# Few-slot experts computed two parts at a time, and the last expert's few-slot tile moved behind the first block's angles

## The chip, the cores and the metric

The kernel runs on one core of one Trainium2 chip. The metric is the time of one execution in microseconds (us); three executions of the kernel before are given, and one further execution was profiled.

## What is computed

Three layers run in one launch: attention with a local window and a few global keys (8 heads, 768 positions, head size 64, batch 2), a mixture of 8 experts in which each of the 1,536 tokens goes to one expert, and a layer that mixes tokens by angles. The change touches the second layer and its border with the third.

```python
# experts: token (b, s) belongs to expert e, with probability p[e]
h = np.maximum(x[b, s] @ w1[e], 0.0)          # 512 -> 1024
out[b, s] = p[e] * (h @ w2[e])                # 1024 -> 512
...
# third layer
theta = x @ w_theta
zr, zi = x * np.cos(theta), x * np.sin(theta)
y = np.einsum('ts,bsd->btd', w_tok_r, zr) + np.einsum('ts,bsd->btd', w_tok_i, zi)
u = x + y
out = u + np.maximum(u @ w_ch, 0.0)
```

All is in float32. A product of two float32 matrices is made in one of two ways: of raw float32 operands in one matmul (which the profile records as two), or of operands split into a high and a low part of type fp32r (three matmuls: high by high, high by low, low by high).

## The kernel before

**Ranks and slots.** The experts are ranked by their number of tokens. Rank r has room for `RCAP[r]` = 288, 256, 256, 256, 192, 192, 160, 160 tokens, in tiles of 128 slots: three tiles for rank 0, two for the others. A last tile with 32 (ranks 0, 6, 7) or 64 (ranks 4, 5) slots is a few-slot tile. `FEW` = 192 is the room up to which the first product of a rank uses raw weights.

**Units.** The 1,024 hidden columns of an expert are cut into 8 parts of 128; one rank and one part are a unit, u = 8 r + f, 64 units in all. For each unit TensorE (PE) runs `mm1(u + 2)` (tokens by w1: 12 fp32r matmuls in ranks 0 to 3, 4 raw ones in ranks 4 to 7), then `mm2(u)` (hidden by w2: for each full tile three fp32r matmuls of 512 columns; for the few-slot tile raw matmuls that put 32 or 64 slots on 32 or 64 columns of the array, 4 or 2 of them side by side, L1501). `relu` makes the hidden parts: ScalarE (ACT) the high part `hh`, VectorE (DVE) the low part `hl` and, for a few-slot tile, the raw `hx`. `split_w1` and `split_w2` split the weights on ACT and DVE. Between these steps `tick` does small steps of the jobs that convert the third layer's 64-bit tables (26 jobs, six steps each, five of them with one DVE operation; `JRATE[r]` steps per unit, until unit `JL`).

**Loads.** SyncE (SP) loads a piece, which is the w1 and the w2 part of two units, 512 KB each, into three buffers each (`raw1`, `raw2`). The next load of a buffer is issued when the last reader of the old piece is done. `x_tr` transposes the tokens of the next rank.

**The border.** After unit 63 `y_last` scales both tiles of rank 7 (full tile on DVE, L1550; few-slot tile on ACT, L1551) and stores them to `yd` with two SP transfers (L1552, L1553). `first_put` puts the first block of 128 tokens together on PE without waiting for the store; then come its angles (L1823), its transposes back (L1827), 8 `keep_warm` matmuls whose result nobody reads (`W0`, L1809), and `h_tr(1)`, the transposes of the second block, which a gather (`gather_y`, on GpSimd, POOL) reads back from `yd`. Then the mix of the first block (L1746) begins.

The order of all instructions is written out by hand: each engine runs its list in the order of the code.

Of the kernel before, what the change touches and what calls it, by code (L numbers as in the profile page):

```python
# [38 lines left out]
FEW = 192  # L39
RBASE = [1, 4, 6, 8, 10, 12, 14, 16]  # L40
NSLOT = 18
LONG = 128 + RCAP[0]
# [22 lines left out]
JRATE = (0, 1.3, 1.3, 1.3, 2.4, 2.4, 2.4, 2.4)  # L65
# [6 lines left out]
JL = 61  # L72
W0, W1 = 8, 0
LOADS = ((1, 1), (0, 2), (1, 2), (2, 1), (2, 2))
# [19 lines left out]
def kernel(  # L94
# [341 lines left out]
    with ExitStack() as actx:  # L436
# [366 lines left out]
        def experts_slots():  # L803
# [20 lines left out]
            V.tensor_scalar(flag_i, ordf[:, 1, 0:1], gA[0:1], None, op0=ALU.max)  # L824
# [10 lines left out]
            V.scalar_tensor_tensor(yidx, slotf[:, 0], 128.0, slotf[:, 1], op0=ALU.add, op1=ALU.add)  # L835

# [142 lines left out]
    xgs, pieces, regs = {}, {}, {}  # L979
    NPC = 32  # L980

    def load_piece(n, parts=(1, 2)):
# [4 lines left out]
        k = r if n else -1  # L987
        if k not in regs:
            regs[k] = SP.value_load(order_g[0:1, r : r + 1] if n else first_i, min_val=0, max_val=E - 1)
        ev = regs[k]  # L990
        p = pieces.setdefault(n, {})
        if 2 not in p and 2 in parts:
            p[2] = pre.tile([128, 2, DM], F32, tag="raw2", name="raw2", bufs=NRAW)
# [34 lines left out]
    slot0 = ct([128, 1], F32, "slot0")  # L1028

# [247 lines left out]
    wsp1, mb_, pR_ = {}, [], []  # L1277
# [9 lines left out]
    def x_tr(r, i, low=True):  # L1287
# [8 lines left out]
        tp = (pR_[0] if r else pZ).tile([128, 4, 128], F32, tag="tr", name="tr")  # L1296
# [45 lines left out]
    with ExitStack() as mctx:  # L1342
# [5 lines left out]
        pR_.append(pR)  # L1348
        pslot = {}
# [11 lines left out]
        def gather_p(r, i):  # L1361
            n = RBASE[r] + i
            pslot[n] = mb.tile([128, 1], F32, tag="ps", name="ps", bufs=6)
# [36 lines left out]
        def first_put():  # L1400

            outs = first["xT"] = [pB.tile([128, 2, 128], F32, tag="b", name="first") for _ in range(2)]
            for n, (rows, pick) in enumerate(((first["rows"], ident), (first["yo"][0], first["hitT"]))):
# [21 lines left out]
        hts = {}  # L1425

        hps = {}

        def mm1(u):
# [4 lines left out]
            hp = pB.tile([128, 512], F32, tag="b", name="h")  # L1434
            if N <= FEW:
                x, o = f32(xTs[r][0]), u % 2
# [10 lines left out]
            else:  # L1447
                h1, l1 = wsp1.pop(u)
# [6 lines left out]
            hps[u] = hp  # L1455

        def relu(u):
            if u >= 64:
                return
            r = u // 8  # L1460
            N = RCAP[r]
            hp = hps.pop(u)
            hh = mb.tile([128, max(RCAP)], F32R, tag="hh", name="hh", bufs=4)
            hl = mb.tile([128, max(RCAP)], F32R, tag="hl", name="hl", bufs=4)
            n, hx = N // 128 * 128, None
            if width(r, RTILES[r] - 1) == 128:
                n = N
            A.activation(hh[:, :n], hp[:, :n], AF.Relu)  # L1468
            if n < N:

                hx = mb.tile([128, 64], F32, tag="hx", name="hx", bufs=4)
                V.tensor_scalar(hx[:, : N - n], hp[:, n:N], 0.0, None, op0=ALU.max)
            V.scalar_tensor_tensor(hl[:, :n], hp[:, :n], 0.0, f32(hh[:, :n]), op0=ALU.max, op1=ALU.subtract)  # L1473
            hts[u] = (hh, hl, hx)

        yps = {}

        def mm2(u):
            r, f = divmod(u, 8)
            if f == 0:  # L1480
                yps[r] = [pO.tile([128, DM], F32, tag="o", name="o") for _ in range(RTILES[r])]
            h2, l2, w = wsp2.pop(u)
            hh, hl, hx = hts.pop(u)
            for i in range(RTILES[r]):
                lo = i * 128
                M = min(128, RCAP[r] - lo)
                out = yps[r][i]
                c = width(r, i)
                if c == 128:
# [8 lines left out]
                else:  # L1498
                    W = 4 * c
                    for g in range(128 // c):  # L1500
                        PE.matmul(  # L1501
                            out[g * c : g * c + M, :W],
                            lhsT=hx[:, :M],
                            rhs=w[:, g * W : (g + 1) * W],
                            start=(f == 0),
                            stop=(f == 7),
                        )
            if u % 2:
                pieces.pop(u // 2)
                load_piece(u // 2 + NRAW, (2,))  # L1510

        def y_out(u):
# [32 lines left out]
        def y_last():  # L1545
            r, w = E - 1, width(E - 1, 1)
# [8 lines left out]

        mm1(0)
        relu(0)
        mm1(1)
        split_w1(2)
        split_w2(0)  # L1560
        relu(1)
        jstate["eng"], jstate["sub"] = A, V
# [428 lines left out]
```

## Time and profile before

| | us |
|---|---|
| median of three runs | 497.88 |
| lowest, highest | 496.69, 499.67 |
| the profiled execution, whole | 495.95 |
| its span, first to last instruction | 494.1 |
| PE busy in the span | 478.5 |
| DVE busy | 353.8 |
| ACT busy | 260.8 |

The profile lists for each engine when an instruction began, what it waited for, and how long it took. A matmul record is pipelined: records overlap, so the time of a step is read from start to start of what follows it. PEld is the loading of the stationary operand, which goes on beside the matmuls.

### The profile page before, as it was taken

The numbers are of one execution on the slowest core, as the hardware profiler recorded it, in microseconds if no ns is written. First come the engines' busy times: TensorE is split into PE (matmuls) and PEld (weight loads), VectorE is DVE, ScalarE is ACT, GpSimd is POOL, SyncE is SP. The second block draws the span as 40 slices with busy tenths as digits, with TensorE's granted clock in tenths as the row PEclk, the third lists the DMA queues.
The fourth block names the chain that finished last, engine by engine and source line by source line (L and its number), as shares of the span: only waits on it lengthen the run. The fifth ranks groups of instructions, "written<-read, shape, count | busy, mean of one in ns | idle before, by whom it ended". The sixth has DMA issues, their size and how long they took to land.

```text
span 494.1 us, 9501 instructions
## 1 busy us (share of the span) xinstructions
PE 478.5 (97%) x3328; PEld 385.0 (78%) x3330; DVE 353.8 (72%) x955; ACT 260.8 (53%) x634; POOL 117.4 (24%) x145
## 2 busy tenths in 40 slices
PE   8998998899999999999999999999999999999994
PEld 4676776678788899987777776888888888888884
DVE  6878878857665878777777888657999795751421
ACT  5977786732455756665455664555655354520300
POOL 4003214234105303021311102303453232430400
PEclk9999999999999999999999999999999999999999
DMA  8967578713949876976888995420012000000122
GB/s 244 350 191 247 178 242 248 227 44 114 337 63 299 287 255 227 303 253 225 297 278 288 305 312 174 142 98 22 23 64 72 15 23 21 2 34 32 34 96 69
DMA packets 62343, 83.18 MB, mean 168 GB/s; under 512 B 6496, under 2 KB 40928, under 8 KB 62288
## 3 DMA queue, kind: packets, MB, share of 16 engines
q1 hardware_dynamic: 53812, 61.97, 39.4%
q10 hardware_dynamic: 5708, 13.50, 8.0%
q0 software_dynamic: 2768, 7.02, 4.6%
q8 instruction: 28, 0.46, 0.4%
q14 instruction: 27, 0.22, 0.1%
HBM read 71.14 MB, written 11.34 MB: 167 GB/s over the span
## 4 chain that ended last, share of the span: by engine, by line
PE 79%; DVE 7%; DMA 6%; ACT 4%; issue 2%; ACTq 0%; SPq 0%; DVEq 0%; POOLq 0%
PE a L1746 21%; PE o L1491 11%; PE h L1454 8%; PE b L1783 7%; PE th L1670 6%; PE h L1438 6%; PE s L547 3%; PE x L626 3%; PE o L1501 3%; PE pt L602 2%; DVE sm L569 2%; DMA yd<-yo 2%; DMA jraw<-in_w_tokT_dram 2%; PE h L757 2%; PE y L768 2%
## 5 line engine op out<-in xcount | busy, mean ns | idle before, releaser
L1746 PE MATMUL a<-wtokr,z 128*128 128x512 f32 x480 | 87.1, 340 | 0.0
L1746 PEld LDWEIGHTS a<-wtokr,z 128*128 128x128 f32 x480 | 73.5, 188 | 10.7
L1491 PE MATMUL o<-w2s,hh 128*128 128x512 f32 x192 | 64.9, 417 | 0.7 <-DVE w2s L1422 0.4
L579 ACT ACTIVATE pr<-sm,st 128x256 f32<-128x256 f32 (+1 forms) x96 | 46.1, 482 | 19.9 <-DVE st L569 19.9
L1422 DVE TENSOR_TENSOR w2s<-raw,w2s 128x512 fp32r<-128x512 f32 x64 | 44.0, 688 | 14.7 <-ACT w2s L1421 14.6
L1454 PE MATMUL h<-xT,w1s 128*128 128x256 f32 (+1 forms) x384 | 53.4, 288 | 1.2 <-DVE w1s L1325 0.6
L1454 PEld LDWEIGHTS h<-xT,w1s 128*128 128x128 f32 x384 | 49.5, 188 | 4.3 <-DVE w1s L1325 1.1
L1438 PE MATMUL h<-xT,raw 128*128 128x192 f32 (+1 forms) x256 | 46.0, 323 | 0.0
L1438 PEld LDWEIGHTS h<-xT,raw 128*128 128x128 f32 x256 | 38.5, 190 | 7.0 <-issue 6.6
L1421 ACT ACTIVATE w2s<-raw 128x512 fp32r<-128x512 f32 x64 | 39.9, 623 | 7.6 <-ACT yo L1537 3.5
L569 DVE CUSTOM_DVE_ANT_0 sm<-s,bias 128x256 f32<-128x256 f32 (+1 forms) x96 | 34.0, 395 | 10.3 <-PE s L547 10.1
L1468 ACT ACTIVATE hh<-h 128x256 fp32r<-128x256 f32 (+1 forms) x64 | 20.8, 324 | 33.8 <-PE h L1454 18.9
L1491 PE MATMUL o<-w2s,hl 128*128 128x512 f32 x96 | 38.0, 395 | 0.0
L1491 PEld LDWEIGHTS o<-w2s,hh 128*128 128x128 f32 x192 | 33.0, 189 | 5.2 <-DVE w2s L1422 1.2
L1012 POOL DMA_INDIRECT xg<-xd,xidx x17 | 16.8, 986 | 85.0 <-PE tr L1299 78.6
L602 PE MATMUL pt<-ident,pr 128*128 128x128 f32 x176 | 26.0, 280 | 4.5 <-DVE xt L652 3.2
L1325 DVE TENSOR_TENSOR w1s<-raw,w1s 128x512 fp32r<-128x512 f32 x32 | 22.1, 690 | 9.6 <-ACT w1s L1324 9.4
L1791 DVE SCALAR_TENSOR_TENSOR ob<-b,xTf 128x512 f32<-128x512 f32 (+1 forms) x16 | 8.8, 556 | 27.6 <-PE b L1783 27.5
L1702 POOL TENSOR_TENSOR si<-si,yg 128x512 f32<-128x512 f32 x10 | 13.4, 1343 | 60.0 <-ACT si L1695 50.8
L1473 DVE SCALAR_TENSOR_TENSOR hl<-h,hh 128x256 fp32r<-128x256 f32 (+1 forms) x64 | 22.4, 350 | 6.0 <-ACT hh L1468 6.0
L602 PEld LDWEIGHTS pt<-ident,pr 128*128 128x128 f32 x176 | 19.2, 141 | 9.4 <-DVE xt L652 3.8
L547 PE MATMUL s<-kall,q 64*128 64x256 f32 (+1 forms) x192 | 25.6, 385 | 0.0
(266 smaller groups left out, 951.3 us busy)
## 6 DMA issues: line engine op xcount, KB each, us to landing
raw<-in_w_dram SPq DMA_DIRECT2D x64, 512.0 KB, 5.2
vv<-in_pack_dram SPq DMA_DIRECT2D x10, 512.0 KB, 5.7
jraw<-in_w_tokT_dram ACTq DMA_DIRECT2D x10, 512.0 KB, 4.7
w<-in_w_dram SPq DMA_DIRECT2D x16, 256.0 KB, 6.6
kall<-in_pack_dram SPq DMA_DIRECT2D x10, 320.0 KB, 4.4
xd<-xt SPq DMA_DIRECT2D x12, 256.0 KB, 2.1
q<-in_pack_dram SPq DMA_DIRECT2D x11, 256.0 KB, 4.5
yd<-yo ACTq DMA_DIRECT2D x11, 256.0 KB, 4.1
```

The costliest lines, as they stand in the source:

```text
L547: PE.matmul(sp[hh][:, 0:W], lhsT=qs[n][half, j], rhs=kall[half, b, j, t * 160 + 160 - W : t * 160 + 160], start=True, stop=True,)
L569: V.tensor_tensor_reduce(out=sm[:, hh, 0:W], in0=ust[u]["s"][hh], in1=bias[:, 2 * j + hh], scale=-0.125, scalar=BIG, op0=ALU.add, op1=ALU.min,
L579: A.activation(pr[:, hh, 0:W], sm[:, hh, 0:W], AF.Exp, bias=st[:, hh : hh + 1], scale=-1.0, accum_out=sums[n][:, 2 * j + hh : 2 * j + hh + 1],
L602: PE.transpose(pt[:, hh, c], pr[:, hh, c * 128 : (c + 1) * 128], ident)
L1421: A.activation(h2, bb[:, o], AF.Copy)
L1422: V.tensor_tensor(l2, bb[:, o], f32(h2), op=ALU.subtract)
L1438: PE.matmul(hp[:, :N], lhsT=pieces[u // 2][1][:, j, o * 128 : (o + 1) * 128], rhs=x[:, j, :N], start=(j == 0), stop=(j == 3),)
L1454: PE.matmul(hp[:, :N], lhsT=wa[:, j], rhs=xa[:, j, :N], start=(k == 0), stop=(k == 11))
L1491: PE.matmul(out[:M], lhsT=ha[:, lo : lo + M], rhs=wa, start=(f == 0 and q == 0), stop=(f == 7 and q == 2),)
L1670: PE.matmul(th, lhsT=xa[:, j], rhs=wa[:, j], start=(n == 0), stop=(n == 11))
L1746: PE.matmul(acc[b][d][o], lhsT=za[:, d * 128 : (d + 1) * 128], rhs=wa[:, lo:hi], start=(t == 0 and n == 0 and (o == 0 or d % 2 == 0)), sto ...
L1783: PE.matmul(op[:, : hi - lo], lhsT=wa[:, d, e * 128 : (e + 1) * 128], rhs=ua[d][:, lo:hi], start=(n == 0), stop=(n == 11),)
```

## The change

Three things change, and some numbers with them.

1. Ranks 4 to 7 are computed two units at a time: `mm1` of two units, `mm2` of two units, then the few-slot matmuls of both (`mm2_few`). One PSUM tile holds the hidden columns of both units, so `relu` is one ACT and two DVE instructions for the two. The few-slot tile of rank 0 too is computed once per two units.
2. The few-slot tile of rank 7 is not computed there. Its hidden parts are kept in `y0`, its raw w2 is loaded into the place of the third layer's `wch` table (`late`), and its 32 matmuls (`y_few`) stand in the place of the 8 `keep_warm` matmuls. Its store follows the first part of the mix, and the gathers of blocks 1 to 3 stand before it. The first block's split parts `xh`, `xl` move from `wch` to tiles of their own.
3. That is allowed where no token of the first four blocks of the first batch lies in that tile: the flag that starts the general path now also rises when the last expert has more than 128 tokens in the first seven blocks (five small DVE instructions in place of one in `experts_slots`).

The numbers: `JRATE` and `JL` (job steps per unit), the order of the first loads (`LOADS`: the w2 part of piece 0 goes ahead of the w1 part of piece 1), and in unit 0 `mm2(0)` stands ahead of `mm1(2)`.

```diff
-JRATE = (0, 1.3, 1.3, 1.3, 2.4, 2.4, 2.4, 2.4)
+JRATE = (0, 1.4, 1.4, 2, 2.3, 2.3, 1.8, 0.6)
-JL = 61
-W0, W1 = 8, 0
-LOADS = ((1, 1), (0, 2), (1, 2), (2, 1), (2, 2))
+JL = 59
+LOADS = ((0, 2), (1, 1), (1, 2), (2, 1), (2, 2))
...
+        if 2 in parts and n >= NPC - 4:
+            if n % 2 == 0:
+                late[0] = res.tile([128, 4, DM], F32, tag=f"wch{n // 2 % 2}", name="late")
+            p[2] = late[0][:, n % 2 * 2 : n % 2 * 2 + 2]
+        elif 2 not in p and 2 in parts:
...
             if N <= FEW:
-                x, o = f32(xTs[r][0]), u % 2
+                if o == 0:
+                    hps[u] = pB.tile([128, 2, 256], F32, tag="b", name="h")
+                hp = hps[u - o][:, o]
...
+        def mm2_few(u, out=None):
+            r = u // 8
+            i = RTILES[r] - 1
+            c, M, out = width(r, i), RCAP[r] - i * 128, out or yps[r][i]
+            for v in (u, u + 1):
+                hx, w = fews.pop(v)
+                for g in range(128 // c if c < 128 else 0):
+                    PE.matmul(out[g * c : g * c + M, : 4 * c], lhsT=hx[:, :M], ...
...
+        def y_few():
+            out = pA_[0].tile([128, 512], F32, tag="a", name="few")
+            yield
+            for u in range(8 * E - 8, 8 * E, 2):
+                mm2_few(u, out)
+            yield
+            W, M = 4 * width(E - 1, 1), RCAP[E - 1] - 128
+            yo = y0[:, 384 : 384 + W]
+            A.activation(yo, out[:, :W], AF.Copy, scale=pslot.pop(RBASE[E - 1] + 1))
+            SP.dma_start(groups_out(YLAST + 128, M, W), yo)
...
-            mm1(u + 2)
-            mm2(u)
...
+            if RCAP[r] > FEW:
+                if u:
+                    mm1(u + 2)
+                mm2(u)
+                if u % 2:
+                    mm2_few(u - 1)
...
+            elif u % 2 == 0:
+                mm1(u + 2)
+                mm1(u + 3)
+                if f == 2 and r < 7:
+                    for i in range(2):
+                        x_tr(r + 1, i)
+                mm2(u)
+                mm2(u + 1)
+                if r < E - 1:
+                    mm2_few(u)
...
-        keep_warm(W0)
+        next(few)
         h_tr(1)
```

On PE in rank 6 (`h<-xT,raw` is `mm1` of one unit, `o<-w2s` the full tile of `mm2`, `o<-raw,hx` the few-slot tile), two units before:

```order
L1438 MATMUL h<-xT_3934,raw_4064 128x160 x4
L1491 MATMUL o<-w2s_4252,hh 128x512
L1491 MATMUL o<-w2s_4253,hh 128x512
L1491 MATMUL o<-w2s_4252,hl 128x512
L1501 MATMUL o<-raw_4071,hx 32x128 x4
L1438 MATMUL h<-xT_4192,raw_4134 128x160 x4
L1491 MATMUL o<-w2s_4281,hh 128x512
L1491 MATMUL o<-w2s_4282,hh 128x512
L1491 MATMUL o<-w2s_4281,hl 128x512
L1501 MATMUL o<-raw_4143,hx 32x128 x4
```

and a pair of units in rank 6 now:

```order
L1459 MATMUL h<-xT_3895,raw_4000 128x160 x8
L1529 MATMUL o<-w2s_4148,hh 128x512
L1529 MATMUL o<-w2s_4149,hh 128x512
L1529 MATMUL o<-w2s_4148,hl 128x512
L1529 MATMUL o<-w2s_4163,hh 128x512
L1529 MATMUL o<-w2s_4164,hh 128x512
L1529 MATMUL o<-w2s_4163,hl 128x512
L1545 MATMUL o<-raw_4012,hx 32x128 x8
```

The same 22 matmuls stand there, with one stretch of 32-column matmuls in place of two. In rank 7 the last of these rows is gone.

On PE at the border (`th` the first block's angles, `b<-ident,xTf` its transposes back, `b<-ident,yg` the second block's transposes, `a` the mix), before:

```order
L1823 MATMUL th<-wth_97,wch_100 128x256 x4
L1827 MATMUL b<-ident,xTf 128x128 x4
L1809 MATMUL wm<-wth_97,wch_99 128x512 x8
L1634 MATMUL b<-ident,yg 128x128 x4
L1746 MATMUL a<-wtok_95,z_4660 128x512
```

and now:

```order
L1901 MATMUL th<-wth_97,xl 128x256 x4
L1905 MATMUL b<-ident,xTf 128x128 x4
L1545 MATMUL few<-late,y_107 32x128 x32
L1716 MATMUL b<-ident,yg 128x128 x4
L1828 MATMUL a<-wtok_95,z_4518 128x512
```

The 32 few-slot matmuls have taken the place of the 8 whose result nobody reads.

## Rows read from the trace of the kernel before

**Rows 1.** The page, part 1: busy time of the engines.

```profile
PE 478.5 (97%) x3328; PEld 385.0 (78%) x3330; DVE 353.8 (72%) x955; ACT 260.8 (53%) x634; POOL 117.4 (24%) x145
```

**Rows 2.** Windows: length, busy PE, PEld, DVE, ACT, POOL, clock, DMA share, GB/s.

```profile
122.00:150.00 28.00, 26.67 (x195) 21.41 (x195) 19.11 (x50) 13.36 (x30) 4.70 (x6) 1.00 0.71 192
196.00:221.50 25.50, 25.50 (x168) 22.75 (x167) 19.96 (x37) 16.88 (x36) 4.26 (x4) 1.00 0.81 270
267.00:280.00 13.00, 13.00 (x97) 9.40 (x94) 11.01 (x30) 7.31 (x16) 1.89 (x2) 1.00 0.93 308
280.00:292.00 12.00, 12.00 (x100) 8.92 (x100) 10.07 (x25) 8.46 (x18) 0.00 (x0) 1.00 0.91 299
```

**Rows 3.** Waits, 221 to 310 us: engine, line, releaser, total, times, longest.

```profile
PEld o L1501 <- issue: 11.0, 30, 0.4
```

**Rows 4.** Timeline of PE in rank 4 or 5: start, time, line, operation, count.

```profile
248.27 0.76 PE L1491 MATMUL o<-w2s,hh 128*128 128x512 f32 x2
...
249.20 0.65 PE L1501 MATMUL o<-raw,hx 128*64 128x256 f32 x4
...
251.05 0.76 PE L1491 MATMUL o<-w2s,hh 128*128 128x512 f32 x2
```

**Rows 5.** The same, two units with 160-token operands, one unit apart.

```profile
287.09 1.35 PE L1438 MATMUL h<-xT,raw 128*128 128x160 f32 x8
...
289.43 1.35 PE L1438 MATMUL h<-xT,raw 128*128 128x160 f32 x8
```

**Rows 6.** The same, end of rank 3: raw `mm1`, no few-slot tile yet.

```profile
224.21 1.46 PE L1438 MATMUL h<-xT,raw 128*128 128x192 f32 x8
...
226.20 0.62 PE L1491 MATMUL o<-w2s,hh 128*128 128x512 f32 x2
...
226.89 1.46 PE L1438 MATMUL h<-xT,raw 128*128 128x192 f32 x8
```

**Rows 7.** Windows of 0.02 us, few-slot matmuls alone: matmuls in flight in brackets.

```profile
249.46:249.48 0.02, 0.02 (x4) 0.00 (x0) 1.00 0.56 205
...
278.96:278.98 0.02, 0.01 (x2) 0.01 (x2) 1.00 0.72 256
...
279.10:279.12 0.02, 0.02 (x7) 0.02 (x4) 1.00 0.69 256
```

**Rows 8.** Timeline of PE at the border.

```profile
308.95 1.16 PE L1405 MATMUL first<-ident,rows 128*128 128x128 f32 x8
...
314.36 2.09 PE L1809 MATMUL wm<-wth,wch 128*128 128x512 f32 x8
316.65 0.63 PE L1634 MATMUL b<-ident,yg 128*128 128x128 f32 x4 [0.20 <-DMA yg<-yd,yidx]
317.03 2.56 PE L1746 MATMUL a<-wtok,z 128*128 128x512 f32 x12
```

**Rows 9.** The chain that ended last, 307 to 322 us: start, time, what.

```profile
308.70 0.76 DVE yo L1550
...
309.48 0.34 SPq L1552
...
309.92 2.53 DMA yd<-yo
...
313.21 3.30 DMA yg<-yd,yidx
```

**Rows 10.** Start of the experts, ACT: the wait for the first w2 part.

```profile
127.99 0.63 ACT L1421 ACTIVATE w2s<-raw 128x512 fp32r<-128x512 f32 x1 [2.36 <-DMA raw<-in_w_dram]
```

**Rows 11.** Transfers issued 244 to 292 us, weights: count, size, median time to landing.

```profile
raw<-in_w_dram SPq DMA_DIRECT2D x19, 512.0 KB, 5.8
```

**Rows 12.** Windows of the third layer, columns as in rows 2.

```profile
408.00:420.00 12.00, 12.00 (x67) 10.29 (x66) 6.07 (x11) 5.77 (x11) 2.72 (x2) 1.00 0.08 22
420.00:432.00 12.00, 12.00 (x65) 10.21 (x65) 9.08 (x10) 7.12 (x12) 4.88 (x4) 1.00 0.01 2
```

**Rows 13.** Groups by line and form: the longest DVE step of a job.

```profile
L398 DVE SCALAR_TENSOR_TENSOR jw<-jraw,jw 128x512 int32<-128x512 int32 x26 | 23.7, 913 | 0.3
```

More of the change, by code (lines that the diff above doesn't have):

```diff
@@ L39 @@
 FEW = 192
+FEW0 = 4
 RBASE = [1, 4, 6, 8, 10, 12, 14, 16]
 NSLOT = 18
+EARLY = 7
 LONG = 128 + RCAP[0]
@@ L1402, in first_put @@
             outs = first["xT"] = [pB.tile([128, 2, 128], F32, tag="b", name="first") for _ in range(2)]
-            for n, (rows, pick) in enumerate(((first["rows"], ident), (first["yo"][0], first["hitT"]))):
+            for n, (rows, pick) in enumerate(((first["rows"], ident), (first["yo"], first["hitT"]))):
                 for j in range(4):
@@ L1447, in mm1 @@
             else:
+                hps[u] = hp = pB.tile([128, 512], F32, tag="b", name="h")
                 h1, l1 = wsp1.pop(u)
@@ L1480, in mm2 @@
             if f == 0:
-                yps[r] = [pO.tile([128, DM], F32, tag="o", name="o") for _ in range(RTILES[r])]
+                yps[r] = [pO.tile([128, DM], F32, tag="o", name="o") for _ in range(RTILES[r] - (r == E - 1))]
             h2, l2, w = wsp2.pop(u)
             hh, hl, hx = hts.pop(u)
+            fews[u] = hx, w
             for i in range(RTILES[r]):
@@ L1497, in mm2 @@
                         )
[L1498 to L1510, printed above, removed]
+        def mm2_few(u, out=None):
[5 more added lines that the diff above has]
+                for g in range(128 // c if c < 128 else 0):
+                    PE.matmul(
+                        out[g * c : g * c + M, : 4 * c],
+                        lhsT=hx[:, :M],
+                        rhs=w[:, 4 * g * c : 4 * (g + 1) * c],
+                        start=(v % 8 == 0),
+                        stop=(v % 8 == 7),
+                    )
         def y_out(u):
@@ L1802 @@
         halves = (slice(0, 256), slice(256, 512))
-        xh, xl = [w[:, 0].rearrange("p (j c) -> p j c", j=4) for w in wch]
-        wm = pA.tile([128, 512], F32, tag="a", name="wm")
-        def keep_warm(n):
-            for _ in range(n):
-                PE.matmul(wm, lhsT=xh[:, 0], rhs=wth[0][:, 0], start=True, stop=True)
+        xh, xl = [hb.tile([128, 4, 128], F32R, tag=n, name=n) for n in ("xh", "xl")]
+        pA_.append(pA)
+        few = y_few()
+        next(few)
         xTb[0] = hb.tile([128, 4, S], F32, tag="xTf", name="xTf")
@@ L1828 @@
         x2s[0] = x.rearrange("p j c -> p (j c)")
-        keep_warm(W0)
+        next(few)
         h_tr(1)
-        keep_warm(W1)
         lo, hi = halves
@@ L1850 @@
         h_mix(0, 0)
+        next(few, None)
         for _ in range(JBUFS):
```

124 lines of the change are left out of this document (80 added, 44 removed).

## The prediction

> **What bounds the kernel now.** I read the busy times first: PE is busy 478.5 of 494.1 us [rows 1], the other engines far less, so only what shortens PE's own list, or makes it wait, counts. Then the windows by stage: in ranks 5 to 7 PE is busy 13.00 of 13 and 12.00 of 12 us at the full clock, and so it is in ranks 2 and 3 and, but for the first microseconds, in rank 0 [rows 2]. "Busy" hides something: the list of waits has PEld idle ahead of the few-slot matmuls for 11.0 us in 30 places, released by nothing but issue [rows 3]. Between a stretch of full-width matmuls and one of 32 or 64 columns the array runs empty, while the records of the last matmuls still cover the gap. The reader should price the few-slot step by the distance of two equal starts, not by its busy time.
>
> **What a few-slot step costs.** At the end of rank 3 a unit has the raw first product, two full tiles and no few-slot tile: 226.89 - 224.21 = 2.68. One full tile in it takes 226.89 - 226.20 = 0.69 [rows 6]. So the first product and one full tile take 1.99, the first product alone 1.30, which is 0.1625 for each of its 8 records of 192 columns; scaled by columns it is 1.08 for 160. A unit of ranks 4 and 5 takes 251.05 - 248.27 = 2.78 [rows 4], so its few-slot step costs 2.78 - 1.99 = 0.79. A unit of ranks 6 and 7 takes 289.43 - 287.09 = 2.34 [rows 5], so there it is 2.34 - 1.08 - 0.69 = 0.57.
>
> **What a second group costs in the same stretch.** No row shows two groups in one stretch. Inside one, the first records of all column groups run together, and their second records begin 0.26 (249.20 to 249.46) and 0.14 (278.97 to 279.10) later [rows 4, 7]; twice that, 0.52 and 0.28, is the upper end, since it holds part of the filling of the array. The lower end is two records in a row at the rate above, 0.43 for 256 columns and 0.22 for 128. I take the middle, 0.475 and 0.25, as neither end is nearer. *TensorE: Matmul & The Clock Gate* of the Trainium skill (Part 3, the span model) says that tiles on different columns run at once and only a few ns apart; by that alone the increment is the lower end and the sum 10.2, while the row's 0.14 speaks for more.
>
> **The change part by part.** *Pairs.* A pair saves 0.79 - 0.475 = 0.315 in ranks 4 and 5: 8 pairs, 2.5 (2.2 to 2.9). In rank 6 it saves 0.57 - 0.25 = 0.32: 4 pairs, 1.3 (1.2 to 1.4). Rank 0's third tile also has 32 slots, and I take the same 1.3 for its 4 pairs.
>
> *Rank 7.* Seven units lose their whole step: 7 x 0.57 = 4.0. The eighth is at the border. The first block's matmuls began at 308.95, 0.25 after DVE could begin on the full tile (308.70) [rows 8, 9]; that 0.25 goes. Then PE spends 0.57 + 7 x 0.25 = 2.32 (2.1 to 2.5) on the few-slot tile where the unread matmuls took 2.09: 0.23 more. So it comes to the second block's transposes at 316.45 - 0.25 + 0.23 = 316.43, by the clock of before, where they began at 316.65 after a wait of 0.20 for the gather [rows 8]. The gather will be there: it now depends on the first store alone, issued at 309.48, not on the second, issued at 309.92 [rows 9], 0.44 earlier. Gain 0.22. With this rank 7 gives 4.2 (3.9 to 4.5).
>
> The sum is 2.5 + 1.3 + 1.3 + 4.2 = 9.3 (8.5 to 10.2).
>
> *Costed at nothing.* The start: ACT waits 2.36 for the first w2 part [rows 10]. It now comes first and the next w1 part second; PE needs both before it can go on for long, and both have landed at the same moment as before. Bounds are that 2.36 either way; I give the range 0.6. The transposes of ranks 5 to 7 are the same matmuls, moved between the two products; the narrow ones may now empty the array on their own, at most 0.57 - 0.22 = 0.35 each, 1.0 in all. The four more DVE instructions of the flag stand behind the token lists, ahead of the split of the first weights, for which DVE waits for a transfer; no row shows them, the nearest, a job's step of 0.91 on 512 columns [rows 13], bounds them at 3.6, and on 8 columns they are far from it. The flag itself cannot rise while the last expert has under 129 tokens; with the reference's inputs it has 96.
>
> The jobs: the rates give 92 steps in place of 101, so 1.5 of 26 jobs move into the third layer, at most 1.5 x 5 x 0.91 = 6.8 of DVE. The cover is PE's mixing: from 408 to 432 us PE is busy 24.00 and DVE 15.15, so 8.8 are free [rows 12, 13]. Were it not for that, 6.8 would show. In rank 3 5.6 more steps, at most 5.1, go on top of DVE's 19.96 of 25.5 [rows 2]: near the edge, and part of the first rival.
>
> The store of the few-slot tile stands on SP behind the gathers of blocks 1 to 3. Queued behind it are the third layer's job loads on SP; on POOL the gather of block 4 waits for it, and behind that the angles' products of block 2. PE wants them two blocks of the mix later. Price if that cover failed: a store and a gather, 2.53 + 3.30 = 5.8 [rows 9]. On ACT the tile's copy moves from ahead of the first block's split to behind the first mix. The moved `xh` and `xl` lie where expert tiles lay; a store still reading there would cost at most its 2.53 [rows 9].
>
> **The rivals.** *The weights or DVE hold the pace (0.17).* The same bytes must come in less time. At 267 to 292 us the DMA engines are busy 0.93 and 0.91 of the time [rows 2]; the pairs there shorten by 0.32 in about 4.9 us, the job rate falls from 2.4 to 2.3 and 1.8 steps, so the share would go to 0.95. If instead the units of ranks 4 to 6 keep their pace, 2.5 + 1.3 are lost and 5.5 remain. Against it: a weight transfer lands in 5.8 [rows 11], and three buffers allow far more (below).
>
> *The stretches don't merge (0.05).* If the array also runs empty between the groups of a pair, since both add to the same accumulators, the pairs give nothing (5.1 lost) and the moved tile pays 7 x 0.32 = 2.2 more: 2.0 remain. Against it: the second records of a group follow the first within one stretch without such a gap [rows 7].
>
> *The clock falls at the border (0.03).* All rows here show the granted clock at 1.00, the 2.4 GHz level, also where few-slot matmuls stand in every unit [rows 2]. If 2.3 us of nothing but narrow matmuls took it to 1.2 GHz, these and the transposes and mix behind them (2.3 + 0.4 + 2.6 [rows 8]) would take twice their time: 5.3 more, 4.0 remain. The Trainium skill, *TensorE: Matmul & The Clock Gate* (Part 1), has the rule: the array keeps the full clock only while it has been active, so dropping matmuls meant to keep it warm speaks against the change. No run so far shows a narrow stretch of that length.
>
> *Slower (0.03).* With three w1 buffers a pair cannot be shorter than a third of landing plus first products. At 5.8 and 2.6 that is 2.8, against the new pair of 2 x 1.99 + 0.79 + 0.475 = 5.25 in ranks 4 and 5 and 2 x 1.77 + 0.57 + 0.25 = 4.36 in rank 6. It binds from a landing of 3 x 5.25 - 2.6 = 13.1, and from some 15.5 it takes 0.8 a pair, which eats the 9.3 over 12 pairs. At 18 a pair of ranks 4 and 5 takes 6.9, 1.6 more than wanted: 8 pairs, 13. That would be 3.6 slower than before. It needs the landing to triple on a share that rises by 0.02.
>
> **How the numbers follow.** The sum is against the profiled execution, 495.95 as a whole (its span 494.1 and 1.85 around it): 486.65. The median of the runs is 1.93 above that execution: 488.6. I predict the middle, 487.6. By the same middle (496.9) the first rival gives 491.4, the second 494.9, the clock 492.9, the slower one 500.5. The forecast has the remaining 0.72. Its own bounds are 8.5 - 0.6 - 1.0 = 6.9 and 10.2 + 0.6 = 10.8, so 485.1 from the profiled execution to 491.0 from the median. To hold 8 in 10 the range must take in the first rival: 485.0 to 492.5. A measurement of this kernel can tell about 0.5% (2.5 us) from no change: the forecast, the first rival and the clock lie beyond that, 0.92; the second within, 0.05; slower 0.03.
>
> **What would show it.** In the profile after: PEld's waits on issue ahead of the few-slot matmuls in about half as many places of ranks 4 to 6 and none in rank 7; two units of ranks 4 and 5 in 5.25 (before 5.56), of rank 6 in 4.36 (4.68), of rank 7 in 2 x 1.77 = 3.54; PE busy throughout; the few-slot tile in about 2.3 at the border with the second block's transposes right behind; the clock at 1.00. I am wrong if a pair of ranks 4 to 6 takes as long as two units did (first rival if first products or splits wait for `raw`, second if nothing does), if rank 7's pairs are longer than 3.8, if PE waits at the border over 0.5, or if PE idles in the third layer, where the moved jobs would be the cause.

## The result and the profile after

The changed kernel takes 490.85 us (median, 490.5 to 491.42), the one before 497.28 (four runs, 495.33 to 499.67): ratio 0.987, 95% interval 0.982 to 0.992. The prediction was 487.6 in 485.0 to 492.5. The profiled execution is 490.5 as a whole with a span of 488.6, 5.5 less than before's 495.95 and 494.1. The forecast had 9.3; 3.8 of it did not come.

The page of after, part 1 (busy time of the engines), answers [rows 1]:

```profile
PE 469.6 (96%) x3322; PEld 387.2 (79%) x3322; DVE 352.8 (72%) x927; ACT 258.2 (53%) x618; POOL 117.4 (24%) x145
```

Waits of after in the window of [rows 3] (engine, line, releaser, total, times, longest):

```profile
PEld o L1545 <- issue: 4.4, 12, 0.4
```

Thirty places have become twelve, one a pair in ranks 4 to 6 and none in rank 7. The timeline of PE gives the lengths, which answer [rows 4, 5] (start, time, line, operation, count; left out are the rows between equal starts):

```profile
247.74 1.08 PE L1545 MATMUL o<-raw,hx 128*64 128x256 f32 x8
...
252.94 1.08 PE L1545 MATMUL o<-raw,hx 128*64 128x256 f32 x8
...
283.97 0.65 PE L1545 MATMUL o<-raw,hx 128*32 128x128 f32 x16
...
288.31 0.65 PE L1545 MATMUL o<-raw,hx 128*32 128x128 f32 x16
```

A pair takes 5.20 in ranks 4 and 5 and 4.34 in rank 6, where two units took 5.56 and 4.68. The steps of the sum hold so far. What did not come is lost in waits and in one place that grew dearer. At the start of the experts, ACT's timeline (the wait ahead of the row and its releaser in brackets):

```profile
128.71 1.15 ACT L1342 ACTIVATE w1s<-raw 128x512 fp32r<-128x512 f32 x2 [1.35 <-DMA raw<-in_w_dram]
```

and PE's, which waits for what ACT makes there:

```profile
129.39 0.40 PE L1476 MATMUL h<-xT,w1s 128*128 128x288 f32 x1 [1.43 <-ACT w1s L1342]
130.12 1.06 PE L1476 MATMUL h<-xT,w1s 128*128 128x288 f32 x6 [0.33 <-DVE w1s L1343]
```

Behind rank 0, ACT's timeline:

```profile
159.22 0.36 ACTq L1579 DMA_DIRECT2D yd<-yo  x1
...
165.91 0.37 ACT L1577 ACTIVATE yo<-o,ps 128x128 f32<-128x128 f32 x1 [2.33 <-DMA yd<-yo]
```

and PE's, some 3 us later:

```profile
168.84 0.66 PE L1317 MATMUL tr<-ident,xg 128*128 128x128 f32 x4 [1.08 <-DVE xT L1299]
```

At the border, the chain that ended last (start, time, what), which answers [rows 9]:

```profile
294.25 0.59 ACT yo L1577
...
295.24 0.38 ACT yo L1577
...
295.63 3.35 DMA yd<-yo
...
299.84 3.62 DMA rows<-yd,yidx
...
303.60 2.02 PE first L1424 x16
```

and PE's timeline, which answers [rows 8]:

```profile
301.57 0.40 PE L1529 MATMUL o<-w2s,hl 128*128 128x512 f32 x1
303.60 1.13 PE L1424 MATMUL first<-ident,rows 128*128 128x128 f32 x8 [1.64 <-DMA rows<-yd,yidx]
...
309.09 1.29 PE L1545 MATMUL few<-late,y 128*32 128x128 f32 x38
310.60 1.04 PE L1545 MATMUL few<-late,y 128*32 128x128 f32 x26 [0.22 <-issue]
311.56 0.66 PE L1716 MATMUL b<-ident,yg 128*128 128x128 f32 x4
311.98 2.55 PE L1828 MATMUL a<-wtok,z 128*128 128x512 f32 x12
```

PE is done with the experts at 301.97 (301.57 + 0.40) and then stands until 303.60, for the gather of the first block's rows. The chain shows why that gather is late: it is issued at 299.84, behind the landing of rank 6's second store (295.63 + 3.35). None of the terms had that wait. Below, the few-slot tile takes 2.47 (309.09 to 311.56), with the second block's transposes right behind it. These 2.47 hold a gap ahead of the row at 310.60, in which PE waits for nothing that the profile shows (`issue`). The same stretch in the trace of the kernel with the early stores and the buffer, an experiment below, has none:

```profile
307.27 1.95 PE L1545 MATMUL few<-late,y 128*32 128x128 f32 x64
309.15 0.66 PE L1723 MATMUL b<-ident,yg 128*128 128x128 f32 x4
309.56 2.55 PE L1835 MATMUL a<-wtok,z 128*128 128x512 f32 x12
```

It takes 1.88 there (307.27 to 309.15), and 1.88 or 1.89 in the traces of six of the kernels below; in these six the mix begins 5.73 to 5.77 behind the first block's angles, and here 6.33. So the gap, from start to start, is 0.6 (2.47 - 1.88) of the 3.8 that did not come in this execution. What causes it stays open.

Set side by side, the two traces give this account on PE (after minus before, us):

| place | difference | step | forecast for the step |
|---|---|---|---|
| first product of rank 0 | -0.16 | chance of the run | |
| end of rank 0, 156 | -0.34 | pairs -1.4, start +1.2 | -1.3, 0 |
| first transposes of rank 3's slots, 189 | +0.14 | the wait at 168.84: +0.5 | 0 |
| first product of rank 7's second pair, 288.9 | -2.89 | ranks 4 to 6: -3.0 | -3.8 |
| end of the last expert, 301.96 | -6.74 | rank 7: -3.85 | -4.0 |
| first block's angles, 305.65 | -5.38 | wait for the rows: +1.64, less 0.25 | -0.25 |
| first mix, 311.98 | -5.05 | few-slot tile 2.47 (1.88 and the gap) for 2.09, less 0.20; 0.15 in smaller steps | +0.03 |
| last matmul | -5.48 | third layer: a wait of 0.69, and 0.1 less in each later block | 0 |

### The profile page after: what moved, and what is told of

Read it like the earlier page. It is cut to its first block, busy times and chain, and to the rows that moved or that the text cites. A ratio compares the mean times of both kernels' runs of the same rounds, so it can differ in the third digit from the quotient of the medians.

```text
span 488.6 us, 9435 instructions
## 1 busy us (share of the span) xinstructions
PE 469.6 (96%) x3322; PEld 387.2 (79%) x3322; DVE 352.8 (72%) x927; ACT 258.2 (53%) x618; POOL 117.4 (24%) x145
## 4 chain that ended last, share of the span: by engine, by line
PE 72%; DVE 10%; ACT 6%; DMA 5%; issue 4%; ACTq 1%; SPq 0%; DVEq 0%; POOLq 0%
PE a L1828 18%; PE o L1529 10%; PE h L1476 8%; PE b L1865 7%; PE th L1752 5%; PE h L1459 5%; PE s L550 3%; PE x L629 3%; PE pt L605 3%; DMA yd<-yo 2%; DVE sm L572 2%; PE o L1545 2%; ACT pr L582 1%; DMA raw<-in_w_dram 1%; DMA xd<-xt 1%
## 5 line engine op out<-in xcount | busy, mean ns | idle before, releaser
L1828 PE MATMUL a<-wtokr,z 128*128 128x512 f32 x480 | 85.9, 337 | 0.0
L1529 PE MATMUL o<-w2s,hh 128*128 128x512 f32 x192 | 62.7, 406 | 0.2
L1441 DVE TENSOR_TENSOR w2s<-raw,w2s 128x512 fp32r<-128x512 f32 x56 | 38.4, 687 | 16.4 <-ACT w2s L1440 11.3
L1459 PE MATMUL h<-xT,raw 128*128 128x192 f32 (+1 forms) x256 | 42.2, 317 | 0.0
L1440 ACT ACTIVATE w2s<-raw 128x512 fp32r<-128x512 f32 x56 | 34.9, 624 | 5.0 <-PE o L1529 2.5
L401 DVE SCALAR_TENSOR_TENSOR jw<-jraw,jw 128x512 int32<-128x512 int32 x26 | 24.8, 955 | 0.3
L403 DVE SCALAR_TENSOR_TENSOR jw<-jraw,jw 128x512 int32<-128x512 int32 x26 | 24.6, 946 | 0.1
```

The source lines that it names most:

```text
L401: V.scalar_tensor_tensor(w, lo, 29, w, op0=ALU.logical_shift_right, op1=ALU.bitwise_or)
L1440: A.activation(h2, bb[:, o], AF.Copy)
L1441: V.tensor_tensor(l2, bb[:, o], f32(h2), op=ALU.subtract)
L1459: PE.matmul(hp[:, :N], lhsT=pieces[u // 2][1][:, j, o * 128 : (o + 1) * 128], rhs=x[:, j, :N], start=(j == 0), stop=(j == 3),)
L1529: PE.matmul(out[:M], lhsT=ha[:, lo : lo + M], rhs=wa, start=(f == 0 and q == 0), stop=(f == 7 and q == 2),)
L1828: PE.matmul(acc[b][d][o], lhsT=za[:, d * 128 : (d + 1) * 128], rhs=wa[:, lo:hi], start=(t == 0 and n == 0 and (o == 0 or d % 2 == 0)), sto ...
```

## The experiments

All are edits of the changed kernel, except one. Times are medians; the kernel before took 498.14 beside the first four, 497.21 beside the next four and 498.02 beside the last four. The first product of rank 0 starts between 121.4 and 124.3 in these profiles, with no edit ahead of it, so a single trace is compared from place to place, and only medians as a whole.

**Rank 6's stores early.**

```diff
             r, f = divmod(u, 8)
-            if f == 7:
+            if u == 8 * E - 10:
+                y_rows(r, 0, RTILES[r])
+            elif r == E - 1 and f < 7 or u == 8 * E - 9:
+                return
+            elif f == 7:
```

> The stores of rank 6's two tiles are issued behind rank 6's last pair instead of inside rank 7's first pair; nothing else is changed. Theory A (the gather of the first block's rows waits for these stores, and rank 7, now shorter, no longer covers it): the two yo on ScalarE move from 294.15 and 295.24 us to about 289, the gather is issued at 298 to 298.5 instead of 299.84, the 1.64 us wait of TensorE ahead of `first` falls to under 0.3, and the kernel takes 1.3 to 1.6 us less than the changed kernel's 490.85: 489.2 to 489.6. Theory B (TensorE would wait there anyway, for the last tile's scaling on VectorE or the transfer's own length): the wait stays above 1.2 and the time within 0.4 us of 490.85.

488.94 us (488.32 to 489.53), 1.9 less. POOL's timeline:

```profile
299.24 0.96 POOL L1404 DMA_INDIRECT rows<-yd,yidx  x1 [0.24 <-issue]
```

and PE's:

```profile
302.74 1.13 PE L1424 MATMUL first<-ident,rows 128*128 128x128 f32 x8 [0.23 <-DMA rows<-yd,yidx]
```

The gather no longer waits for a store, and PE's wait falls from 1.64 to 0.23. Theory B is out. In this trace the gain from rank 6's last stretch on is 1.5 (0.67 behind at 288.98, 0.86 ahead at `first`), the size of the wait. Only 0.86 of it is an earlier `first`; the rest is a later end of rank 6, which covers a part of the gather.

**The old start.**

```diff
-LOADS = ((0, 2), (1, 1), (1, 2), (2, 1), (2, 2))
+LOADS = ((1, 1), (0, 2), (1, 2), (2, 1), (2, 2))
...
         mm1(1)
+        split_w1(2)
         split_w2(0)
...
-                if u:
-                    mm1(u + 2)
+                mm1(u + 2)
                 mm2(u)
...
-                if u == 0:
-                    split_w1(2)
-                    mm1(2)
```

> The start of rank 0 as in the kernel before: the load of the second w1 piece ahead of the first w2 piece, and the third first-layer unit ahead of the first second-layer unit. Theory A (the new start costs about 1.2 us by 131 us, but the gap is taken up again at 169 us, where TensorE waits for a store's landing by way of ScalarE's third yo): the wait of 1.43 us at 129.4 goes, TensorE is 1.0 to 1.4 us earlier at 150 us, the wait at 168.8 grows from 1.08 to 1.5 to 2.3, and the whole changes by 0 to -0.5 us: 490.3 to 490.9. Theory B (the loss at the start is carried to the end): 489.4 to 489.8.

490.46 us, but its runs lie from 487.36 to 492.91, so the whole decides nothing. The trace does: from the first product of rank 0 to the first transposes of rank 1 it takes 18.2 where the changed start takes 19.4, and the wait at 168.8 stays at 1.1. It does not take the gain up; I had expected it to grow.

**A buffer of its own for rank 0's third output tile**, so that ACT need not wait for a store to land:

```diff
-                yo = mb.tile([128, DM], F32, tag="yo", name="yo", bufs=2)
+                if r == 0 and i == 2:
+                    yo = res.tile([128, 4, DM], F32, tag="wch0", name="yo")[:, 0]
+                else:
+                    yo = mb.tile([128, DM], F32, tag="yo", name="yo", bufs=2)
```

> Rank 0's third (few-slot) output tile gets a buffer of its own, so that ScalarE need not wait for the first store of rank 0 to land; nothing else is changed. Theory A (rank 0's gain from the pairs is lost in that wait): ScalarE's wait of 2.33 us ahead of the third yo goes, TensorE's wait of 1.08 us at 168.8 for the transposed slots falls to under 0.3, and the kernel takes 0.7 to 1.1 us less than 490.85: 489.8 to 490.2. Theory B (the weights' pace takes it: the next TensorE wait is for w1s or w2s of rank 1): the wait at 168.8 moves to a w1s or w2s within 10 us behind it, and the time stays within 0.4 us of 490.85.

488.1 us (487.31 to 488.34), 2.75 less, more than expected. ACT's timeline, to be read against 165.91 of after:

```profile
162.03 0.36 ACT L1580 ACTIVATE yo<-o,ps 128x128 f32<-128x128 f32 x1
```

The wait is gone, and so is PE's at the transposes. Between the end of rank 0 and rank 4 this trace gains 1.37 on the changed kernel's. A later 0.97 is given back at 266 to 267 us, to waits for `hl` and `w2s`; the wait for the rows, 0.62 instead of 1.64, makes that up. Why the median gains 2.75 I cannot show.

**The three together.**

> The three edits together: rank 6's stores early, the old start, and the buffer of its own for rank 0's third tile. Theory A (the three losses are separate, and all lie on the path): 1.5 from the stores, 1.0 from the buffer and 1.2 from the start, 3.2 to 3.8 us less than 490.85: 487.0 to 487.7, TensorE ahead of the changed kernel by 2.0 to 2.4 us at 180 us. Theory B (weights and slots arrive at a pace of their own in ranks 0 and 1): the stores' gain alone, 489.2 to 489.6.

486.82 us (486.02 to 486.83), 4.0 less than the changed kernel and a ratio of 0.977 (0.974 to 0.981) to the one before: the fastest kernel here. Theory B is out; the time is a little below theory A's 487.0 to 487.7. Alone the three edits gave 1.9, 0.4 and 2.75, 5.1 in all, so they are not quite separate.

**The early stores and the buffer, with the changed start.**

> The changed kernel with rank 6's stores early and the buffer of its own for rank 0's third tile, but with the changed start: what it takes beside the kernel with all three edits (486.82) is the price of the new start alone. Theory A (the new start costs 0.9 to 1.2 us, which stay): a wait of 0.9 to 1.4 us for w1s at about 129 us, and 487.6 to 488.0. Theory B (the start's loss is taken up by later waits): 486.6 to 487.1.

487.9 us (486.78 to 488.6) against 486.82: the new start costs 1.1 by the medians, as theory A has it, though the two sets of runs touch. The trace has the wait for w1s at 1.3, and the first pair of rank 0 ends 12.56 behind rank 0's first product, with the three edits together 11.46. This distance varies from run to run: 11.97 to 12.64 in the eight traces with the changed start, 10.96 to 11.98 in the four of pairs with the old one, 0.9 apart on average. The early stores, worth 1.9 alone, add only 0.2 to the kernel with the buffer (488.1 to 487.9): these two gains overlap.

**The buffer in the kernel before.** The same edit there.

> The kernel before, with the same buffer of its own for rank 0's third tile. Theory A (the wait behind that store was in the kernel before too, 1.11 us on ScalarE and 0.8 on TensorE, and varies with the store's landing): the two waits at 168 to 169 us go, the kernel is 0.8 to 1.6 us faster than the one before, and its times lie closer together than the 4.6 us over which those of before are spread. Theory B (the wait is new with the change): no difference from the kernel before.

496.55 us, ratio 0.999 (0.997 to 1.001): no difference, and the spread (495.24 to 500.46) stays. In the trace 0.75 is gained between 168 and 189 and 0.66 lost again in rank 7. So this wait was in the kernel before too, but taking it away brings nothing there that can be measured; theory A had that wrong, and the spread of the kernel before has another cause, which stays open.

**Stretches unpaired in ranks 4 to 6.** `mm2_few` takes the number of its units as `k`; in part:

```diff
                 mm2(u)
+                if r < E - 1:
+                    mm2_few(u, k=1)
                 mm2(u + 1)
                 if r < E - 1:
-                    mm2_few(u)
+                    mm2_few(u + 1, k=1)
```

> In ranks 4 to 6 the few-slot matmuls of a pair are no longer in one stretch: each unit's eight stand behind that unit's own second-layer matmuls, as before the change; the first-layer stretches of two units, the transposes, rank 0 and rank 7 stay as changed. Theory A (a stretch has a fixed price of about 0.35 us beside its own 0.22 or 0.43, which the pair saves once): each of the 12 pairs is 0.30 to 0.35 us longer (5.50 to 5.56 instead of 5.20 in ranks 4 and 5, about 4.66 instead of 4.34 in rank 6), rank 7 begins 3.6 to 4.2 us later against rank 4's begin, and the kernel takes 494.3 to 495.2. Theory B (the gain of the pairs comes from the two units' first-layer matmuls standing together and from the single relu, not from the stretch): pairs stay at 5.2 to 5.3, 490.5 to 491.5.

491.86 us (490.52 to 493.71), only 1.0 more, where 3.4 to 4.4 were expected. Waits in the window of [rows 3]:

```profile
PEld o L1545 <- issue: 8.0, 22, 0.4
```

and PE's timeline, two equal starts of rank 4 or 5 and the border:

```profile
243.47 2.87 PE L1459 MATMUL h<-xT,raw 128*128 128x192 f32 x16
...
249.03 2.87 PE L1459 MATMUL h<-xT,raw 128*128 128x192 f32 x16
...
304.36 1.13 PE L1424 MATMUL first<-ident,rows 128*128 128x128 f32 x8 [0.40 <-DMA rows<-yd,yidx]
```

A pair takes 5.56 again, and over the twelve pairs 3.8 are lost (1.14 ahead of the changed kernel at rank 4, 2.63 behind it at the end of rank 6). So the stretch's price is what the pairs save, as theory A has it. But behind rank 6 the loss shrinks to 0.76 at `first`: 0.38 because rank 7 has no wait for `w2s`, and 1.24 because the wait for the rows is 0.40 instead of 1.64; the rest is in smaller steps that I did not trace. At the mix only 0.16 are left (312.14), since the few-slot tile runs without the gap here. What ranks 4 to 6 gain or lose comes through the border only in part.

**Rank 7's few-slot matmuls twice.** In `mm2` rank 7 gets its second output tile again, `mm2_few` leaves its operands in place for the second time, and:

```diff
-                if r < E - 1:
-                    mm2_few(u)
+                mm2_few(u)
+                if r < E - 1:
                     pieces.pop(u // 2)
```

> Rank 7's few-slot matmuls are done twice: as changed behind the first block's angles, and a second time in pairs inside rank 7, into a tile that nothing reads. Theory A (rank 7 on TensorE sets the end of the experts, except for the first 1.6 us, in which the rows' gather is late): each pair of rank 7 is 0.75 to 0.8 us longer, 3.0 to 3.2 in all, the wait ahead of `first` goes, and the kernel takes 1.3 to 1.7 us more: 492.1 to 492.6. Theory B (rank 7 is set by the weights or by VectorE): under 0.5 us more. Theory C (the wait for the rows doesn't shrink when rank 7 grows): 3.0 or more, 493.9.

493.42 us (491.53 to 494.6), 2.6 more. PE's timeline at the border:

```profile
303.45 1.16 PE L1424 MATMUL first<-ident,rows 128*128 128x128 f32 x8
...
312.17 0.63 PE L1716 MATMUL b<-ident,yg 128*128 128x128 f32 x4 [1.22 <-DMA yg<-yd,yidx]
```

Rank 7's part from 287.64 to 303.45 is 15.81 for 13.08, 2.7 longer. The wait for the rows goes, as theory A says; theories B and C are out. The extra 1.22 is a wait that none of the three had: the gather of the second block's rows, which stands on the last expert's store.

**A quarter of the few-slot tile at the border.**

```diff
-            for u in range(8 * E - 8, 8 * E, 2):
-                mm2_few(u, out)
+            mm2_few(8 * E - 2, out)
...
-                        start=(v % 8 == 0),
+                        start=(v % 8 == (6 if u == 8 * E - 2 else 0)),
```

> Of rank 7's few-slot tile only the last of its four pairs of units is computed behind the first block's angles (16 of 64 matmuls, the rest of that tile's sum is left out); nothing takes the place of the other 48. Theory A (the tile is done in TensorE's wait for the angles, off the path; the clock holds without it): TensorE waits some 1.9 us there, the granted clock stays at 1.00 up to 330 us, the first mixing matmuls start at the same distance behind `th` (6.3 us), and the time is 490.2 to 491.2. Theory B (the few-slot tile lies on the path): the first mixing matmuls start 0.5 to 1.9 us earlier, 489.0 to 490.3. Theory C (the tile keeps the clock up): the granted clock falls below 1.00 in the stretch behind the wait, 491.5 or more.

489.37 us, from 486.74 to 490.51. PE's timeline at the border:

```profile
310.24 0.64 PE L1545 MATMUL few<-late,y 128*32 128x128 f32 x16
311.25 0.63 PE L1715 MATMUL b<-ident,yg 128*128 128x128 f32 x4 [0.37 <-issue]
312.43 2.40 PE L1827 MATMUL a<-wtok,z 128*128 128x512 f32 x12 [0.55 <-ACT z L1802]
```

and two windows there (length, busy PE, PEld, DVE, ACT, POOL, clock, DMA share, GB/s):

```profile
310.00:314.00 4.00, 3.08 (x32) 2.21 (x31) 3.65 (x12) 3.45 (x9) 0.99 (x2) 1.00 0.68 186
314.00:320.00 6.00, 6.00 (x35) 5.12 (x34) 2.35 (x6) 1.87 (x5) 0.00 (x0) 1.00 0.79 268
```

The times spread too far to decide. In the trace the mix begins 5.64 behind `th` (306.79) where the changed kernel has 6.33. That is 0.69 less, within theory B's 0.5 to 1.9. But against the six traces in which the whole tile runs without the gap, 5.73 to 5.77, it is 0.1 less. So without the gap nearly all of the three quarters left out is off the path, as theory A has it; the 1.9 us wait of A didn't appear, since PE takes the next transposes at once and then waits for `z`. The clock stays at 1.00: C is out.

**Transposes behind the few-slot stretch.**

```diff
-                if f == 2 and r < 7:
-                    for i in range(2):
-                        x_tr(r + 1, i)
                 mm2(u)
                 mm2(u + 1)
                 if r < E - 1:
                     mm2_few(u)
+                    for i in range(2 if f == 2 else 0):
+                        x_tr(r + 1, i)
```

> The transposes of the next rank's slots in ranks 4 to 6 stand right behind a few-slot stretch, as they did before the change, instead of between the first-layer and the second-layer matmuls; nothing else is changed. Theory A (transposes beside a few-slot stretch share its fixed price, and cost 0.77 us a pair there against 1.02 where they stand now): each of the three pairs with transposes is 0.2 to 0.3 us shorter, TensorE is 0.6 to 0.9 us earlier at the end of rank 6, of which the wait for the first block's rows takes up half or more: 490.1 to 490.8 in all. Theory B (the price belongs to the eight transposes, wherever they stand): the pairs with transposes stay at 6.2 us, 490.5 to 491.2.

494.76 us (493.23 to 496.02): 3.9 more, which neither theory had. PE's timeline in rank 4:

```profile
238.53 1.04 PE L1317 MATMUL tr<-ident,xg 128*128 128x128 f32 x8
239.51 2.87 PE L1459 MATMUL h<-xT,raw 128*128 128x192 f32 x16
...
243.21 0.50 PE L1529 MATMUL o<-w2s,hl 128*128 128x512 f32 x1 [0.37 <-issue]
...
244.41 0.50 PE L1529 MATMUL o<-w2s,hh 128*128 128x512 f32 x1 [0.47 <-DVE w2s L1441]
```

ACT's there:

```profile
239.23 0.87 ACT L1320 ACTIVATE xT<-tr 128x512 f32<-128x512 f32 x2 [4.66 <-PE tr L1317]
239.98 0.63 ACT L1440 ACTIVATE w2s<-raw 128x512 fp32r<-128x512 f32 x1
```

and ACT's at the same place of after:

```profile
235.47 0.87 ACT L1320 ACTIVATE xT<-tr 128x512 f32<-128x512 f32 x2 [2.10 <-PE tr L1317]
```

The eight transposes (the row counts four of 128x128 and four of 64x64 together) take 0.98 there (238.53 to 239.51), against 0.92 between the products: nothing is shared, and theory A falls. The loss has another way: ACT's list has the copy of the transposes ahead of the next pair's `w2s`. When the transposes come later on PE, ACT waits 4.66 for them with nothing else to do, the split behind it is late, and PE waits for it in the next pair. Rank 4's two pairs take 12.76 (232.31 to 245.07) for 11.42.

**The four edits together.**

> The four edits together: rank 6's stores early, the old start, the buffer of its own, and the transposes behind the few-slot stretch. Theory A (with the stores early the end of rank 7 sets the time again, so the 0.6 to 0.9 us of the transposes arrive): 486.0 to 486.4, against 486.82 for the first three. Theory B (waits for w2s, or the rows' gather, take it): 486.6 to 487.0.

492.4 us (491.57 to 495.59), 5.6 more than the first three: the same loss. Its trace has 2.1 of PE waits for DVE's `w2s` and 0.9 for ACT's.

**The four, with fewer job steps in rank 5.**

```diff
-JRATE = (0, 1.4, 1.4, 2, 2.3, 2.3, 1.8, 0.6)
+JRATE = (0, 1.4, 1.4, 2, 2.3, 1.7, 1.8, 0.6)
```

> The four edits, and in rank 5 the steps of the background jobs come at 1.7 instead of 2.3 a unit, so that less of them stands ahead of the weights' splitting on ScalarE and VectorE. Theory A (TensorE's waits for w2s in ranks 5 to 7, 1.0 us in all, come from the jobs): the waits fall under 0.4 us, TensorE is 0.4 to 0.7 us earlier at the end of rank 7, and the five or so steps that are left over cost nothing behind it: 485.4 to 486.1. Theory B (the steps left over are on the path behind the experts): the same gain, lost again by the end, 486.2 to 487. Theory C (the waits come from the weights' transfers): the waits stay.

496.65 us (494.91 to 499.07), 4.2 more than without it. DVE's waits fall from 2.1 to 0.7 and `first` comes 1.8 earlier than with the four edits, so most of the waits come from the jobs, as theory A says. But then, PE's timeline in the third layer:

```profile
377.95 3.80 PE L1831 MATMUL a<-wtokr,z 128*128 128x256 f32 x11 [3.75 <-ACT wtokr L408]
```

and the windows behind it (columns as above):

```profile
378.00:380.00 2.00, 1.89 (x6) 1.44 (x7) 0.62 (x1) 0.00 (x0) 0.00 (x0) 0.70 0.87 340
380.00:382.00 2.00, 2.00 (x8) 1.66 (x7) 0.43 (x1) 0.00 (x0) 0.00 (x0) 0.50 0.04 10
382.00:384.00 2.00, 2.00 (x10) 1.64 (x9) 0.27 (x1) 0.00 (x0) 0.00 (x0) 0.95 0.00 0
384.00:386.00 2.00, 2.00 (x13) 1.70 (x12) 0.00 (x0) 1.16 (x3) 0.00 (x0) 1.00 0.00 0
```

A job's result is not there when the mix wants it, PE stands for 3.75, and behind that the granted clock is 0.70, 0.50 (the 1.2 GHz level) and 0.95 in three windows of 2 us. Theory B, at a price that it had much too low: the mix to the last matmul takes 5.1 longer.

## Why the prediction was right, and where its sum was wrong

The direction and the range were right, and so was the mechanism of the pairs; the sum was 3.8 too high against the profiled execution, and its likeliest time 3.2 too low. The hit owes something to luck: 490.85 lies 0.15 inside the sum's own upper bound of 491.0, and nearer to the first rival's 491.4 than to 487.6. The traces part the two, since the pairs did shorten, which that rival excludes; losses elsewhere add up to much the same time. Three of the prediction's own signs of being wrong appeared: PE waited 1.64 at the border (0.5 was the bound), one pair of rank 7 took 3.92 (292.56 to 296.48; the bound was 3.8), and PE waited in the third layer.

**Pairs.** A plain pair of ranks 4 and 5 gains 0.36 for the forecast 0.315, of rank 6 0.34 for 0.32. The stretch of two groups takes 1.01 and 0.57 where one took 0.58 and 0.36 (starts in the timelines), so the second unit's costs 0.43 and 0.21: the lower end. The 0.14 between second records, which made me take the middle, was no sign of a dearer second group. Here the span model of *TensorE: Matmul & The Clock Gate* in the Trainium skill (Part 3), which gave that end, agrees with the trace. The rival of stretches that don't merge is out: undone, the pairs are at 5.56 again.

**Transposes, costed at nothing.** The step fails. PE's timeline of after, rank 4:

```profile
231.11 1.08 PE L1545 MATMUL o<-raw,hx 128*64 128x256 f32 x8
...
234.83 0.99 PE L1317 MATMUL tr<-ident,xg 128*128 128x128 f32 x8
...
237.33 1.08 PE L1545 MATMUL o<-raw,hx 128*64 128x256 f32 x8
```

Two tiles' transposes cost 1.02 a pair (6.22 against 5.20, from the starts of the stretches) where before they cost 0.39 and 0.38, apart. Three such pairs are some 0.7, inside the bound of 1.0 that the text gave; the value taken, nothing, was wrong. The price is the eight transposes' own (the row counts four of 128x128 and four of 64x64 together), 0.92 to 0.98 in both places tried; why they were cheaper one tile at a time is not shown. Moved elsewhere they cost more, for ACT's sake.

**The start, costed at nothing.** The step fails. That both parts are there at the same moment as before is roughly true: ACT begins on the second one 6.03 behind rank 0's first product where it was 5.15 (5.36 to 6.03 in the eight traces with the changed start, 4.65 to 5.68 in the six with the old). And the part that comes second, w1's, has a split on ACT and another on DVE ahead of its product, while PE has no work to put in between. Together it costs about 1: 1.1 by the medians of two kernels that differ in nothing else, 0.9 on average over the traces. The text's own range for it was 0.6.

**Rank 0.** Its pairs gain 1.4 for 1.3: the last three take 20.63 (135.32 to 155.95) for 21.65, 0.34 each, and the first, which the start hides, is taken as the same. Behind it 0.5 are lost, as the store at 159.22 took 6.61 to land (before 5.49, chain of waits), and ACT, PE's transposes and their copies follow each other from there. With a buffer of its own the changed kernel gains 2.75, the kernel before nothing. That the wait holds the changed kernel is shown; how much of the 3.8 it is, beyond the 0.5 of this trace, is not.

**Rank 7 and the border.** Rank 7 gains 3.85 for the 4.0 of its first seven units; one wait of 0.37 at 295.42, inside a row, is more than the difference. The 0.25 behind the last tile went as forecast. The few-slot tile takes 2.47 for 2.32, but by the six traces without the gap its own size is 1.88: that term was too high, and the gap hid it. What failed is that I followed only one gather at the border, that of the second block. The first block's rows are gathered too, behind rank 6's stores; before, they had been asked for at 302.66 and were needed at 308.95, so the chain showed no wait, and the 4 us that rank 7 lost were its cover. This is the missing term, 1.64 in the trace and 1.9 by the median of the kernel with the early stores; in the five other traces with the late stores and rank 7 as changed the wait is 0.40 to 0.80. It is also why gains of ranks 4 to 6 arrive only in part.

**The rivals.** The weights did not hold the pace: windows of after in 267 to 292 us have the DMA share at 0.93 and 0.91, the same as [rows 2], and PE busy 12.86 of 13 and 12.00 of 12. (These windows hold the end of rank 5 and rank 6, not ranks 5 to 7 as the prediction says.) DVE and ACT cost a part of it, in two waits for `w2s` of about 0.4 each (268 and 295 us); the last experiment speaks for the jobs as their cause. The clock at the border stayed at 1.00, with the tile and with a quarter of it. In the third layer, while matmuls were left, it fell in the last experiment alone, behind 3.75 us without a matmul. That is the case of which Part 1 of the same page of the Trainium skill warns, and the border was not one. But it also fell far ahead of the change, in the attention layer, in three of the fourteen traces (the early stores, the early stores and the buffer, the transposes behind the stretch). Windows of the second of these (columns as in [rows 2]):

```profile
44.00:46.00 2.00, 2.00 (x22) 1.50 (x22) 1.63 (x11) 2.00 (x8) 0.00 (x0) 0.73 0.98 272
46.00:48.00 2.00, 2.00 (x18) 1.50 (x16) 0.38 (x3) 0.88 (x2) 0.00 (x0) 0.50 1.06 248
```

Ahead of them PE waits 1.5 for DVE, as it does in all fourteen traces; why the clock falls in three of them is open. Nothing was slower.

**The jobs moved into the third layer, costed at nothing.** The step fails here too, though by less: PE waits 0.69 where before it had no wait. Its timeline and DVE's, of after:

```profile
341.84 2.10 PE L1752 MATMUL th<-wth,xh 128*128 128x512 f32 x8 [0.69 <-DVE rr L1766]
339.95 0.69 DVE L411 TENSOR_TENSOR wtokr<-jw,wtokr 128x512 fp32r<-128x512 f32 x1 [0.70 <-ACT wtokr L408]
```

Four steps of a job (337.12 to 339.95) stand on DVE's list ahead of the angles' `rr` there, where the kernel before had one. That the layer as a whole is 0.43 shorter all the same is owed to its later blocks, 11.57 each for 11.69, from the starts of their angles; why they are shorter is open. I had counted DVE's free time from 408 to 432 us; the last experiment shows that a job's result has a due time at 374 us, where DVE is busy 28.89 of 30 (340 to 370 us of after). Some five steps more, and PE stands. What covered the jobs was the order of the results, not the free time behind it. The price of 0.91 a step was a mean, too: the two longest steps of a job take 0.68 in ranks 4 to 7 and up to 1.67 and 1.78 in the third layer (343.85 and 346.50 of after).

The best kernel here keeps the change and takes the start and the two stores out of its way: 486.82, near the 486.65 of the sum, though by another account.

## What to carry to other kernels

When a stage becomes shorter, list every transfer that the next stage reads, not only the one that was late: each had the old length of the stage as its cover. An instruction that is moved on one engine is also moved for the copy that waits for it on another, and what is queued behind that copy is late with it. Work that is put off is covered by the time at which its result is wanted, not by free time anywhere behind.

## What the runs showed of the hardware

Four transposes of 128x128 and four of 64x64 cost 0.92 to 0.98 us in one stretch, the first four alone 0.39 in a unit of the kernel before (234.53 to 237.70, less 2.78). The few-slot matmuls of a second unit in a stretch cost two more records (0.43 and 0.21), and the fixed price of a stretch is then 0.15 (0.58 - 0.43 and 0.36 - 0.21) inside it and 0.2 more around it, 0.36 and 0.34 in all as the pairs show. A store of 256 KB took from 5.5 to 6.6 us to land behind rank 0, one of 64 KB 3.35 at the border. The granted clock was 1.00 behind PE's waits of 1.43 and 1.64 in the changed kernel, and down to 0.50 behind the one of 3.75 in the last experiment; behind one of 1.5 at 43 us it stayed at 1.00 in eleven traces and fell to 0.50 in three. The start of the experts moves by up to 2.9 us from run to run in profiles with no edit ahead of it. Where the clock falls at 44 us, that is a part of it: two places that lie 5.22 apart in the changed kernel (43.85 and 49.07) lie 6.56 apart (43.04 and 49.60) with the early stores and the buffer, 1.3 more. The rest is open.
